# One exponential in seven computed on VectorE instead of ScalarE, with a new schedule for the background work

## The chip, the cores and the metric

The kernel runs on one core of a Trainium2 chip. The metric is device time in microseconds (us) for one execution. Engines are named as the profile names them: PE is TensorE (PEld its weight loads), ACT is ScalarE, DVE is VectorE, POOL is GpSimd. PSUM is the memory that holds PE's results. A bank is here a PSUM tile of 512 fp32 columns on 128 partitions; both kernels use eight.

## The reference

Two transformer layers on x of shape 1 x 2048 x 512 in bf16, with 32 heads of 16 columns and a feed-forward part of 1792 columns. Both layers use the same weights.

```python
x = A_x
x = x + attention(layernorm(x), A_wqkv, A_wo)   # softmax(q k^T * 16**-0.5) v, 32 heads
x = x + ffn(layernorm(x), B_w1, B_w2)           # silu between two matmuls
x = x + attention(layernorm(x), A_wqkv, A_wo)
x = x + ffn(layernorm(x), B_w1, B_w2)
```

## The kernel before

The scores of one head are cut into blocks of 128 keys x 512 queries. There are 2 layers x 4 query chunks x 4 groups x 2 parities x 16 key tiles x 4 heads = 4096 blocks. Sixty-four blocks (16 key tiles x 4 heads j) share one accumulator `o_ps`; I call them a group, so there are 64 groups. The main loop takes three blocks a step. PE computes three scores (each on one quarter of the array's rows, because a head's keys have 32 rows with padding), ACT takes the exponential of all three in one instruction, and two steps later PE multiplies the result with the values (each on one quarter of the columns).

```python
NB = 3
ps_s = tile_pool(name="ps_s", bufs=2, space=PSUM)   # 2 x 3 banks of scores
ps_o = tile_pool(name="ps_o", bufs=1, space=PSUM)   # 1 bank: the group's accumulator
ps_m = tile_pool(name="ps_m", bufs=1, space=PSUM)   # 1 bank: everything else
# ... cut ...
for t, blks in enumerate(tiles):                    # 1366 steps
    # ... ensure that q, k, v of these blocks are there ...
    s_ps = ps_s.tile([P, NB, 512], FP32, name="s_ps", tag="s")
    for i, (L, qc, g, par, kt, j) in enumerate(blks):
        nc.tensor.matmul(s_ps[:, i, :], lhsT=KT[...][r, ...], rhs=QT[L, qc][r, g, par, :], ...)
    if t >= 2:
        emit_pv(t - 2)                              # value products into o_ps
    nc.scalar.activation(p_tiles[t][...], s_ps[...], ACT.Exp, scale=SCALE)
    if urgent:
        run_urgent()                                # a finished group: divide, transpose, store
    else:
        bg.pump()                                   # one piece of background work
```

Everything else is background work: projections, output projection, layer norms and the feed-forward part are Python generators, and `bg.pump()` emits the next piece of one of them into the engines' streams. `yield None` ends a piece in the middle of a unit. `yield n` ends a unit and skips n steps before the next piece. The whole unit goes through the single `ps_m` bank.

```python
def ffn(L, c, emit):
    # ... cut ...
    for ft in range(FT):
        # four matmuls into h_ps, with `yield None` after the second
        nc.scalar.activation(t_sb[:], h_ps[:], ACT.Tanh, scale=0.5)
        nc.vector.scalar_tensor_tensor(out=hT[:, ft, :], in0=t_sb[:], scalar=1.0, in1=h_ps[:], ...)
        yield 1
    # ... the units of the other generators end with `yield 0`
```

The softmax here doesn't subtract the row's maximum and nothing guards it: scores larger than these inputs give would overflow.

## Time and profile before

| | before |
|---|---|
| time, median of 4 runs | 2280.52 us (2278.79 to 2282.66) |
| exponentials | 1366 of 1536 columns (the last of 512) |
| ACT busy | 1915.0 us, 84% |
| PE busy, mean granted clock | 1856.3 us, 0.718 |
| DVE busy | 414.4 us, 18% |

The first fence holds the busy line and the chain that ended last, from the page. The chain is followed back from the last instruction, and the line with the largest share is where time can be gained first.

```profile
PE 1856.3 (81%) x10240; PEld 537.5 (24%) x10240; DVE 414.4 (18%) x746; ACT 1915.0 (84%) x1479; POOL 36.4 (2%) x47
...
ACT 42%; PE 26%; issue 22%; DVE 9%; POOL 0%; DMA 0%; ACTq 0%; POOLq 0%; DVEq 0%
ACT p_sb L467 39%; PE s_ps L456 6%; PE o_ps L399 5%; PE h_ps L310 4%; ACT t_sb L320 3%; PE q_ps L214 2%; DVE QT L224 2%; PE f_ps L334 2%; PE v_ps L235 2%; DVE oT L408 2%; PE k_ps L197 2%; PE t_ps L177 1%; PE att L253 1%; DVE hT L321 1%; DVE st L152 1%
```

ACT, and on it the exponential, leads. The groups of before, from the page, give the busy time and mean duration of a line, then the idle time of its engine just ahead of it and what ended that.

```profile
L467 ACT ACTIVATE p_sb<-s_ps 128x1536 bf16<-128x1536 f32 x1366 | 1867.9, 1536 | 237.0 <-PE s_ps L456 235.8
L456 PE MATMUL s_ps<-QT,KT 32*128 32x512 bf16 x4096 | 705.4, 504 | 180.2 <-ACT p_sb L467 162.6
L399 PE MATMUL o_ps<-p_sb,VA 128*32 128x512 bf16 x4096 | 732.5, 514 | 42.6 <-DVE oT L408 42.3
```

ACT was busy with exponentials for 1867.9 us and stood idle 237.0 us ahead of them.

The timeline of before at a quiet place (no background work) shows PE alone. Columns are start, length, engine, line, tile.

```profile
1300.07 0.61 PE L456 MATMUL s_ps<-QT,KT 32*128 32x512 bf16 x3 [0.19 <-ACT p_sb L467]
1300.61 0.61 PE L399 MATMUL o_ps<-p_sb,VA 128*32 128x512 bf16 x3
1301.41 0.61 PE L456 MATMUL s_ps<-QT,KT 32*128 32x512 bf16 x3 [0.18 <-ACT p_sb L467]
```

Three scores take one slot of 0.54 us (start to start) together, three products another, and then PE waits for ACT. ACT sets the pace at 1.34 us a step. PE runs these in the order in which the program emits them: in the whole trace of before, three scores and three products alternate (1362 and 1363 times), apart from the first steps and the last. The view in stretches gives busy time of each engine and the granted clock: the two attention loops (first to last finished group of a layer), then a quiet stretch of five groups.

```profile
113.00:1086.00 973.00, 824.38 (x4826) 235.23 (x4825) 180.60 (x320) 919.91 (x704) 13.36 (x15) 0.75 0.00 1
1222.00:2189.00 967.00, 815.19 (x4603) 229.37 (x4600) 121.90 (x226) 916.18 (x703) 3.80 (x6) 0.68 0.01 2
1253.00:1401.00 148.00, 127.15 (x659) 33.42 (x657) 6.87 (x15) 143.08 (x108) 0.00 (x0) 0.50 0.00 1
```

The columns are the stretch, its length, busy us (and instructions) of PE, PEld, DVE, ACT and POOL, then the granted PE clock, DMA share and GB/s. In the quiet stretch PE is granted half its clock.

### The profile page before, as it was taken

How to read it: one execution, taken by the hardware profiler on the slowest of the kernel's cores; microseconds unless marked ns; L12 is line 12 of the kernel's file. 1: busy time of each engine (PE TensorE's matmuls, PEld its weight loads, DVE VectorE, ACT ScalarE, POOL GpSimd, SP SyncE). 2: the span in 40 equal slices, each digit the busy share in tenths (PEclk: the TensorE clock that was granted, in tenths of full speed). 3: DMA queues.
4: the chain of work that ended last, by engine and by line, in shares of the span. 5: the costliest groups of instructions: out<-in, count | busy, mean ns of one | idle time of the engine just before them, and what ended most of it. 6: DMA issues, size and time to landing. Idle time of an engine off the chain costs nothing.

```text
span 2279.7 us, 24321 instructions
## 1 busy us (share of the span) xinstructions
PE 1856.3 (81%) x10240; PEld 537.5 (24%) x10240; DVE 414.4 (18%) x746; ACT 1915.0 (84%) x1479; POOL 36.4 (2%) x47
## 2 busy tenths in 40 slices
PE   5788888888888888788657888878888788888866
PEld 1222222222222222222222222222222222222222
DVE  4430012130312112120221000311012100210021
ACT  1499999999899989999407999899989899999941
POOL 1100000000000000000000000000000000000000
PEclk9995567985779767985666555799567965787556
DMA  4000000000000000000000000000000000000000
GB/s 138 0 1 1 1 1 1 1 1 1 1 1 1 1 1 1 1 1 1 1 0 1 1 1 1 1 1 10 1 1 1 8 3 1 1 1 10 1 0 9
DMA packets 7917, 11.51 MB, mean 5 GB/s; under 512 B 384, under 2 KB 6784, under 8 KB 7808
## 3 DMA queue, kind: packets, MB, share of 16 engines
q1 hardware_dynamic: 7808, 9.96, 1.3%
q8 instruction: 80, 1.31, 0.2%
q14 instruction: 29, 0.24, 0.0%
HBM read 7.86 MB, written 2.10 MB: 4 GB/s over the span
## 4 chain that ended last, share of the span: by engine, by line
ACT 42%; PE 26%; issue 22%; DVE 9%; POOL 0%; DMA 0%; ACTq 0%; POOLq 0%; DVEq 0%
ACT p_sb L467 39%; PE s_ps L456 6%; PE o_ps L399 5%; PE h_ps L310 4%; ACT t_sb L320 3%; PE q_ps L214 2%; DVE QT L224 2%; PE f_ps L334 2%; PE v_ps L235 2%; DVE oT L408 2%; PE k_ps L197 2%; PE t_ps L177 1%; PE att L253 1%; DVE hT L321 1%; DVE st L152 1%
## 5 line engine op out<-in xcount | busy, mean ns | idle before, releaser
L467 ACT ACTIVATE p_sb<-s_ps 128x1536 bf16<-128x1536 f32 x1366 | 1867.9, 1536 | 237.0 <-PE s_ps L456 235.8
L456 PE MATMUL s_ps<-QT,KT 32*128 32x512 bf16 x4096 | 705.4, 504 | 180.2 <-ACT p_sb L467 162.6
L399 PE MATMUL o_ps<-p_sb,VA 128*32 128x512 bf16 x4096 | 732.5, 514 | 42.6 <-DVE oT L408 42.3
L456 PEld LDWEIGHTS <-KT 32*128 32x128 bf16 x4096 | 222.7, 95 | 724.7 <-issue 707.3
L399 PEld LDWEIGHTS <-VA 128*32 128x32 bf16 x4096 | 144.9, 98 | 500.2 <-issue 500.2
L310 PE MATMUL h_ps<-fT,w_sb 128*128 128x512 bf16 x448 | 171.1, 486 | 62.8 <-DVE hT L321 60.2
L408 DVE CAST oT<-o_ps 128x512 bf16<-128x512 f32 x64 | 44.1, 689 | 755.9 <-PE o_ps L399 755.5
L320 ACT ACTIVATE t_sb<-h_ps 128x512 f32<-128x512 f32 x112 | 73.5, 657 | 105.9 <-PE h_ps L310 105.9
L321 DVE SCALAR_TENSOR_TENSOR hT<-t_sb,h_ps 128x512 bf16<-128x512 f32 x112 | 77.0, 688 | 389.1 <-ACT t_sb L320 389.1
L334 PE MATMUL f_ps<-w_sb,hT 128*128 128x512 bf16 x448 | 129.6, 394 | 10.7 <-DVE hT L321 4.8
L310 PEld LDWEIGHTS <-w_sb 128*128 128x128 bf16 x448 | 39.3, 109 | 146.5 <-issue 142.2
L224 DVE TENSOR_SCALAR QT<-q_ps,mask 128x512 bf16<-128x512 f32 x64 | 45.1, 746 | 142.4 <-PE q_ps L214 142.4
L177 PE MATMUL t_ps<-ident,xn 128*128 128x128 bf16 x256 | 36.2, 308 | 38.7 <-DVE xn L163 33.2
L235 PE MATMUL v_ps<-w_qkv,xnT 128*128 128x512 bf16 x128 | 51.7, 530 | 18.4 <-DVE VA L244 12.7
L343 DVE SCALAR_TENSOR_TENSOR x_sb<-f_ps,x_sb 128x512 bf16<-128x512 f32 x32 | 22.1, 692 | 216.6 <-PE f_ps L334 216.6
L214 PE MATMUL q_ps<-xnT,w_qkv 128*128 128x512 bf16 x128 | 48.4, 470 | 14.9 <-DVE QT L224 13.8
L253 PE MATMUL att<-ident,oT 128*128 128x128 bf16 x256 | 34.8, 281 | 30.4 <-DVE hT L321 11.2
L197 PE MATMUL k_ps<-xnT,w_qkv 128*128 128x512 bf16 x128 | 46.3, 463 | 10.3 <-DVE xnT L182 3.9
L334 PEld LDWEIGHTS <-hT 128*128 128x128 bf16 x448 | 32.6, 99 | 67.8 <-issue 52.3
L289 PE MATMUL y_ps<-wo_sb,aT 128*128 128x512 bf16 x128 | 43.0, 427 | 4.6 <-DVE aT L283 1.6
L152 DVE BATCH_NORM_STATS2 st<-x_sb 128x6 f32<-128x512 bf16 x64 | 42.7, 667 | 3.1 <-DMA x_sb<-in_A_x_dram 3.1
L253 PEld LDWEIGHTS <-oT 128*128 128x128 bf16 x256 | 20.8, 120 | 88.0 <-issue 65.1
(30 smaller groups left out, 319.9 us busy)
## 6 DMA issues: line engine op xcount, KB each, us to landing
w_sb<-in_B_w_dram SPq DMA_DIRECT2D x2, 1792.0 KB, 14.2
x_sb<-in_A_x_dram SPq DMA_DIRECT2D x4, 512.0 KB, 8.8
out_dram<-x_sb SPq DMA_DIRECT2D x16, 128.0 KB, 1.7
w_qkv<-in_A_wqkv_dram SPq DMA_DIRECT2D x1, 1536.0 KB, 7.4
wo_sb<-in_A_wo_dram SPq DMA_DIRECT2D x1, 512.0 KB, 9.5
```

The source lines that it names most:

```text
L197: nc.tensor.matmul(k_ps[:], lhsT=w_qkv[:, ct, D + P * g : D + P * (g + 1)], rhs=xnT[L, c][:, ct, :], start=(ct == 0), stop=(ct == CT - 1),)
L214: nc.tensor.matmul(q_ps[:], lhsT=w_qkv[:, ct, P * g : P * (g + 1)], rhs=xnT[L, c][:, ct, :], start=(ct == 0), stop=(ct == CT - 1),)
L224: nc.vector.tensor_scalar_mul(out=QT[L, c][:, g, par, :], in0=q_ps[:], scalar1=masks[par][:, 0:1])
L235: nc.tensor.matmul(v_ps[:], lhsT=xnT[L, c][:, ct, tq * P : (tq + 1) * P], rhs=w_qkv[:, ct, 2 * D : 3 * D], start=(ct == 0), stop=(ct == CT ...
L310: nc.tensor.matmul(h_ps[:], lhsT=w1_sb[:, ct, ft * P : (ft + 1) * P], rhs=fT[:, ct, :], start=(ct == 0), stop=(ct == CT - 1),)
L320: nc.scalar.activation(t_sb[:], h_ps[:], ACT.Tanh, scale=0.5)
L321: nc.vector.scalar_tensor_tensor(out=hT[:, ft, :], in0=t_sb[:], scalar=1.0, in1=h_ps[:], op0=ALU.add, op1=ALU.mult,)
L334: nc.tensor.matmul(y_ps[:], lhsT=hT[:, ft, tq * P : (tq + 1) * P], rhs=w2_sb[:, ft, :], start=(ft == 0), stop=(ft == FT - 1),)
L399: nc.tensor.matmul(o_ps[32 * j : 32 * j + 32, :], lhsT=VA[L, kt // 4][:, kt % 4, 17 * h : 17 * h + 32], rhs=p_sb[:, i, :], start=(kt == 0) ...
L408: nc.vector.tensor_copy(out=oT[:], in_=o_ps[:])
L456: nc.tensor.matmul(s_ps[:, i, :], lhsT=KT[L, kt // 4][r, g, (kt % 4) * P : (kt % 4 + 1) * P], rhs=QT[L, qc][r, g, par, :], start=True, sto ...
L467: nc.scalar.activation(p_tiles[t][:, 0:n, :].rearrange("p a b -> p (a b)"), s_ps[:, 0:n, :].rearrange("p a b -> p (a b)"), ACT.Exp, scale= ...
```

## The change

The intent is to take exponentials off ACT. In a step with three ACT blocks a fourth block now goes to DVE, as long as it lies before place 54 of its group. That makes 9 of 64 blocks, 576 in all. The code uses no exponential instruction on DVE; it builds the exponential out of the number format. An affine writes 1024 (x + const), with x the score in units of log2, into uint16. Read as fp16 these bits are y = 2^e (1+m), where x = e + m. Two bitwise ops cut out 2^e (as fp16) and r = 1+m. Then r (A + C r^2) 2^e, added to 2^e, is close to a constant times 2^x. The addition is not done on DVE: PE accumulates both parts with the same values, in two value products.

The fourth block needs a PSUM bank. The kernel keeps to eight, so the score tiles shrink from 3+3 to 3+2 banks and the exponentials alternate between three blocks and two. Apart from this the schedule of the background work changes: units skip a step, a further step lies between the matmuls of h and their tanh, a finished group is divided one step later, the queries of the next chunk are projected group by group, and the background piece is emitted ahead of the step's exponential instead of after it. The sizes of some buffer pools change too (queries, x, tanh).

```diff
-    NB = 3
+    D_LAST = 54
-    ps_s = ctx.enter_context(tc.tile_pool(name="ps_s", bufs=2, space=bass.MemoryType.PSUM))
+    ps_s = ctx.enter_context(tc.tile_pool(name="ps_s", bufs=1, space=bass.MemoryType.PSUM))
@@ every generator but the layer norm
-        yield 0
+        yield 1
@@ ffn
+            yield None
             t_sb = tpool.tile([P, 512], FP32, name="t_sb", tag="t")
             nc.scalar.activation(t_sb[:], h_ps[:], ACT.Tanh, scale=0.5)
@@ steps
-    tiles = [blocks[i : i + NB] for i in range(0, len(blocks), NB)]
+        n = 3 - len(steps) % 2
+        a = blocks[pos : pos + n]
+        pos += n
+        d = blocks[pos : pos + 1] if n == 3 and pos % 64 < D_LAST else []
@@ the moved block: emit_d, then one stage of step_d a step (cut)
+        s_ps = ps_s.tile([P, 512], FP32, name="d_ps", tag="sd")
+        score(blk, s_ps[:])
+        nc.vector.tensor_scalar(out=pr["y"][...], in0=s_ps[:], scalar1=..., scalar2=..., op0=mult, op1=add)
+            nc.vector.tensor_scalar(out=rf.bitcast(I32), in0=y.bitcast(I32), scalar1=0x03FF03FF, scalar2=0x3C003C00, op0=bitwise_and, op1=bitwise_or)
+            nc.vector.tensor_scalar(out=ef.bitcast(I32), in0=y.bitcast(I32), scalar1=0x7C007C00, op0=bitwise_and)
+                nc.vector.tensor_tensor(out=rf, in0=rf, in1=rf, op=ALU.mult)
+                nc.vector.tensor_scalar(out=rf, in0=rf, scalar1=EXP_C, scalar2=EXP_A, op0=ALU.mult, op1=ALU.add)
+                nc.vector.tensor_tensor(out=rf, in0=rf, in1=y.bitcast(FP16), op=ALU.mult)
@@ value products of a moved block: two, the e part and the r part
+                    blk, [pr["e"][:, i, :].bitcast(FP16), pr["r"][:, i, :].bitcast(FP16)]
@@ main loop
+            run_d()
+            if not run_urgent(t):
+                bg.pump()
             p_tiles[t] = ppool.tile(...)
             nc.scalar.activation(...)
-            if urgent:
-                run_urgent()
-            else:
-                bg.pump()
```

More of the change, by code (lines that the diff above doesn't have):

```diff
@@ L1 @@
+import math
 from collections import deque
@@ L13 @@
 FP32 = mybir.dt.float32
+FP16 = mybir.dt.float16
+U16 = mybir.dt.uint16
+I32 = mybir.dt.int32
 BF16 = mybir.dt.bfloat16
@@ L87 @@
     VW = 17 * H + 16
-    NB = 3
+    EXP_K = 4.58045666e-01
+    SHIFT = -math.log2(EXP_K)
+    EXP_A = 4.65708474e-01 / EXP_K
+    EXP_C = 7.62931392e-02 / EXP_K
+    D_LAST = 54
     const = ctx.enter_context(tc.tile_pool(name="const", bufs=1))
@@ L94 @@
     vpool = ctx.enter_context(tc.tile_pool(name="vpool", bufs=7))
-    qpool = ctx.enter_context(tc.tile_pool(name="qpool", bufs=2))
-    xtpool = ctx.enter_context(tc.tile_pool(name="xtpool", bufs=5))
+    qpool = ctx.enter_context(tc.tile_pool(name="qpool", bufs=6))
+    xtpool = ctx.enter_context(tc.tile_pool(name="xtpool", bufs=4))
     ftpool = ctx.enter_context(tc.tile_pool(name="ftpool", bufs=1))
     xnpool = ctx.enter_context(tc.tile_pool(name="xnpool", bufs=4))
-    ppool = ctx.enter_context(tc.tile_pool(name="ppool", bufs=4))
+    ppool = ctx.enter_context(tc.tile_pool(name="ppool", bufs=2))
+    dpool = ctx.enter_context(tc.tile_pool(name="dpool", bufs=2))
     opool = ctx.enter_context(tc.tile_pool(name="opool", bufs=2))
@@ L102 @@
     hpool = ctx.enter_context(tc.tile_pool(name="hpool", bufs=1))
-    tpool = ctx.enter_context(tc.tile_pool(name="tpool", bufs=2))
+    tpool = ctx.enter_context(tc.tile_pool(name="tpool", bufs=1))
     small = ctx.enter_context(tc.tile_pool(name="small", bufs=3))
-    ps_s = ctx.enter_context(tc.tile_pool(name="ps_s", bufs=2, space=bass.MemoryType.PSUM))
+    ps_s = ctx.enter_context(tc.tile_pool(name="ps_s", bufs=1, space=bass.MemoryType.PSUM))
     ps_o = ctx.enter_context(tc.tile_pool(name="ps_o", bufs=1, space=bass.MemoryType.PSUM))
@@ L206, in proj_k @@
         nc.vector.tensor_copy(out=KT[L, c][:, g, :], in_=k_ps[:])
-        yield 0
+        yield 1
     def proj_q(L, c, g):
-        if g == 0:
-            QT[L, c] = qpool.tile([P, NG, 2, 512], BF16, name="QT", tag="QT")
+        QT[L, c, g] = qpool.tile([P, 2, 512], BF16, name="QT", tag="QT")
         q_ps = ps_m.tile([P, 512], FP32, name="q_ps", tag="m")
@@ L224, in proj_q @@
             nc.vector.tensor_scalar_mul(
-                out=QT[L, c][:, g, par, :], in0=q_ps[:], scalar1=masks[par][:, 0:1]
+                out=QT[L, c, g][:, par, :], in0=q_ps[:], scalar1=masks[par][:, 0:1]
             )
-        yield 0
+        yield 1
     def proj_v(L, c):
@@ L247, in proj_v @@
             )
-            yield 0
+            yield 1
     def group_out(L, qc, g, par, oT):
@@ L283, in out_proj @@
             nc.vector.tensor_copy(out=aT[:], in_=a_ps[:])
-            yield 0
+            yield 1
             for u in range(2):
@@ L300, in out_proj @@
                 )
-                yield 0
+                yield 1
     def ffn(L, c, emit):
@@ L352, in ffn @@
                 nc.sync.dma_start(of[tt * P : (tt + 1) * P, :], x_sb[:, tt, :])
-            yield 0
+            yield 1
     def add_qkv(L, c):
@@ L359, in add_qkv, with next_q @@
         bg.add(("v", L, c), proj_v(L, c))
-    def add_q(L, c):
-        for g in range(NG):
+    def next_q(L, c, g):
+        L, c = (L, c + 1) if c + 1 < NC else (L + 1, 0)
+        if L < 2:
             bg.add(("q", L, c, g), proj_q(L, c, g))
@@ L374 @@
     blocks = list(stream())
-    tiles = [blocks[i : i + NB] for i in range(0, len(blocks), NB)]
-    o_tiles = {}
+    steps = []
+    pos = 0
+    while pos < len(blocks):
+        n = 3 - len(steps) % 2
+        a = blocks[pos : pos + n]
+        pos += n
+        d = blocks[pos : pos + 1] if n == 3 and pos % 64 < D_LAST else []
+        pos += len(d)
+        steps.append((a, d))
+    o_tiles = {}
+    o_count = {}
+    o_total = {}
+    for a, d in steps:
+        for blk, m in [(b, 1) for b in a] + [(b, 2) for b in d]:
+            o_total.setdefault(blk[0:4], [0] * 4)[blk[5]] += m
     p_tiles = {}
+    pairs = deque()
     def start_chunk(L, qc):
         attn[L, qc] = apool.tile([P, 4, D], BF16, name="attn", tag="attn")
-        if qc + 1 < NC and (L, qc) != (1, 0):
-            add_q(L, qc + 1)
-        if (L, qc) == (0, NC - 1):
-            add_q(1, 0)
     def finish_chunk(L, qc):
@@ L390, in finish_chunk, with pv_block @@
             add_qkv(1, qc)
-    def emit_pv(tile_i):
-        p_sb = p_tiles.pop(tile_i)
-        for i, (L, qc, g, par, kt, j) in enumerate(tiles[tile_i]):
-            if kt == 0 and j == 0:
-                o_tiles[L, qc, g, par] = ps_o.tile([P, 512], FP32, name="o_ps", tag="o")
-            o_ps = o_tiles[L, qc, g, par]
-            h = 8 * g + 2 * j + par
-            nc.tensor.matmul(
-                o_ps[32 * j : 32 * j + 32, :],
-                lhsT=VA[L, kt // 4][:, kt % 4, 17 * h : 17 * h + 32],
-                rhs=p_sb[:, i, :],
-                start=(kt == 0),
-                stop=(kt == NKT - 1),
-            )
-            if kt == NKT - 1 and j == 3:
-                oT = opool.tile([P, 512], BF16, name="oT", tag="oT")
-                nc.vector.tensor_copy(out=oT[:], in_=o_ps[:])
-                urgent.append(((L, qc, g, par), group_out(L, qc, g, par, oT)))
+    def pv_block(blk, rhs):
+        L, qc, g, par, kt, j = blk
+        h = 8 * g + 2 * j + par
+        return [((L, qc, g, par), j, VA[L, kt // 4][:, kt % 4, 17 * h : 17 * h + 32], p) for p in rhs]
@@ new lines, in emit_pv @@
+    def emit_pv(mms):
+        mms = list(mms)
+        while mms:
+            used = set()
+            for mm in list(mms):
+                key, j, lhsT, rhs = mm
+                if j in used:
+                    continue
+                used.add(j)
+                mms.remove(mm)
+                if key not in o_tiles:
+                    o_tiles[key] = ps_o.tile([P, 512], FP32, name="o_ps", tag="o")
+                    o_count[key] = [0] * 4
+                n = o_count[key]
+                n[j] += 1
+                nc.tensor.matmul(
+                    o_tiles[key][32 * j : 32 * j + 32, :],
+                    lhsT=lhsT,
+                    rhs=rhs,
+                    start=(n[j] == 1),
+                    stop=(n[j] == o_total[key][j]),
+                )
+        if o_count[key] == o_total[key]:
+            oT = opool.tile([P, 512], BF16, name="oT", tag="oT")
+            nc.vector.tensor_copy(out=oT[:], in_=o_tiles[key][:])
+            urgent.append((key, group_out(*key, oT), step_now[0] + 1))
@@ new lines, in emit_d @@
+    def emit_d(blk):
+        s_ps = ps_s.tile([P, 512], FP32, name="d_ps", tag="sd")
+        score(blk, s_ps[:])
+        if not pairs or len(pairs[-1]["blks"]) == 2 or pairs[-1]["last"]:
+            pairs.append(
+                dict(
+                    blks=[],
+                    stage=0,
+                    last=False,
+                    y=dpool.tile([P, 2, 512], U16, name="d_y", tag="y"),
+                )
+            )
+        pr = pairs[-1]
+        nc.vector.tensor_scalar(
+            out=pr["y"][:, len(pr["blks"]), :],
+            in0=s_ps[:],
+            scalar1=float(1024 * SCALE * math.log2(math.e)),
+            scalar2=float(1024 * (15 - SHIFT)),
+            op0=ALU.mult,
+            op1=ALU.add,
+        )
+        pr["blks"].append(blk)
+        pr["last"] = 4 * blk[4] + blk[5] + 6 >= D_LAST
@@ new lines, in step_d @@
+    def step_d(pr):
+        n = len(pr["blks"])
+        y = pr["y"][:, 0:n, :].rearrange("p a b -> p (a b)")
+        if pr["stage"] == 0:
+            e = dpool.tile([P, 2, 512], U16, name="d_e", tag="e")
+            r = dpool.tile([P, 2, 512], U16, name="d_r", tag="r")
+            pr["e"], pr["r"] = e, r
+            ef = e[:, 0:n, :].rearrange("p a b -> p (a b)")
+            rf = r[:, 0:n, :].rearrange("p a b -> p (a b)")
+            nc.vector.tensor_scalar(
+                out=rf.bitcast(I32),
+                in0=y.bitcast(I32),
+                scalar1=0x03FF03FF,
+                scalar2=0x3C003C00,
+                op0=ALU.bitwise_and,
+                op1=ALU.bitwise_or,
+            )
+            nc.vector.tensor_scalar(
+                out=ef.bitcast(I32),
+                in0=y.bitcast(I32),
+                scalar1=0x7C007C00,
+                scalar2=None,
+                op0=ALU.bitwise_and,
+            )
+        else:
+            rf = pr["r"][:, 0:n, :].rearrange("p a b -> p (a b)").bitcast(FP16)
+            if pr["stage"] == 1:
+                nc.vector.tensor_tensor(out=rf, in0=rf, in1=rf, op=ALU.mult)
+                nc.vector.tensor_scalar(
+                    out=rf, in0=rf, scalar1=EXP_C, scalar2=EXP_A, op0=ALU.mult, op1=ALU.add
+                )
+            else:
+                nc.vector.tensor_tensor(out=rf, in0=rf, in1=y.bitcast(FP16), op=ALU.mult)
+        pr["stage"] += 1
@@ new lines, in run_d, with ready_d @@
+    def run_d():
+        for pr in pairs:
+            if pr["stage"] > 0 or len(pr["blks"]) == 2 or pr["last"]:
+                if pr["stage"] < 3:
+                    step_d(pr)
+                else:
+                    pr["stage"] += 1
+    def ready_d():
+        mms = []
+        while pairs and pairs[0]["stage"] >= 4:
+            pr = pairs.popleft()
+            for i, blk in enumerate(pr["blks"]):
+                mms += pv_block(
+                    blk, [pr["e"][:, i, :].bitcast(FP16), pr["r"][:, i, :].bitcast(FP16)]
+                )
+        return mms
@@ L411, with score @@
+    def score(blk, out):
+        L, qc, g, par, kt, j = blk
+        r = slice(32 * j, 32 * j + 32)
+        nc.tensor.matmul(
+            out,
+            lhsT=KT[L, kt // 4][r, g, (kt % 4) * P : (kt % 4 + 1) * P],
+            rhs=QT[L, qc, g][r, par, :],
+            start=True,
+            stop=True,
+        )
     urgent = deque()
+    step_now = [0]
     with tc.manual_schedule(
@@ L427, with run_urgent @@
             bg.add(("q", 0, 0, g), proj_q(0, 0, g))
-        def run_urgent():
-            bg.close()
-            while urgent:
-                key, gen = urgent.popleft()
-                for _ in gen:
-                    pass
-                bg.done.add(("g",) + key)
-                L, qc, g, par = key
-                if (g, par) == (NG - 1, 1):
-                    finish_chunk(L, qc)
-                    if (L, qc) == (0, NC - 1):
-                        add_q(1, 1)
-        for t, blks in enumerate(tiles):
-            for L, qc, g, par, kt, j in blks:
+        def run_urgent(t):
+            if not urgent or bg.inside or urgent[0][2] > t:
+                return False
+            key, gen, _ = urgent.popleft()
+            for _ in gen:
+                pass
+            L, qc, g, par = key
+            if (g, par) == (NG - 1, 1):
+                finish_chunk(L, qc)
+            return True
+        late = []
+        for t, (a_blks, d_blks) in enumerate(steps):
+            for L, qc, g, par, kt, j in a_blks + d_blks:
                 if (g, par, kt, j) == (0, 0, 0, 0):
                     start_chunk(L, qc)
+                if (par, kt, j) == (0, 0, 0) and (L, qc, g) != (0, 0, 0):
+                    pg = (L * NC + qc) * NG + g - 1
+                    next_q(pg // (NC * NG), pg // NG % NC, pg % NG)
                 if j == 0 and kt % 4 == 0:
@@ L452 @@
                         bg.ensure(("v", L, c))
-            s_ps = ps_s.tile([P, NB, 512], FP32, name="s_ps", tag="s")
-            for i, (L, qc, g, par, kt, j) in enumerate(blks):
-                r = slice(32 * j, 32 * j + 32)
-                nc.tensor.matmul(
-                    s_ps[:, i, :],
-                    lhsT=KT[L, kt // 4][r, g, (kt % 4) * P : (kt % 4 + 1) * P],
-                    rhs=QT[L, qc][r, g, par, :],
-                    start=True,
-                    stop=True,
-                )
-            if t >= 2:
-                emit_pv(t - 2)
-            n = len(blks)
-            p_tiles[t] = ppool.tile([P, NB, 512], BF16, name="p_sb", tag="p")
+            n = len(a_blks)
+            size = 3 - t % 2
+            s_ps = ps_s.tile([P, size, 512], FP32, name="s_ps", tag=f"s{size}")
+            for i, blk in enumerate(a_blks):
+                score(blk, s_ps[:, i, :])
+            for blk in d_blks:
+                emit_d(blk)
+            step_now[0] = t
+            mms, late = late, []
+            if t >= 0:
+                mms += ready_d()
+                for u in (t - 2,):
+                    if u >= 0:
+                        p_sb = p_tiles.pop(u)
+                        for i, blk in enumerate(steps[u][0]):
+                            mms += pv_block(blk, [p_sb[:, i, :]])
+            if mms:
+                key = min(mm[0] for mm in mms)
+                late = [mm for mm in mms if mm[0] != key]
+                emit_pv([mm for mm in mms if mm[0] == key])
+            run_d()
+            if not run_urgent(t):
+                bg.pump()
+            p_tiles[t] = ppool.tile([P, size, 512], BF16, name="p_sb", tag=f"p{size}")
             nc.scalar.activation(
@@ L472 @@
             )
-            if urgent:
-                run_urgent()
-            else:
-                bg.pump()
-        for t in range(len(tiles) - 2, len(tiles)):
-            emit_pv(t)
-        run_urgent()
+        t = len(steps)
+        while p_tiles or late:
+            step_now[0] = t
+            mms, late = late, []
+            for u in sorted(p_tiles):
+                p_sb = p_tiles.pop(u)
+                for i, blk in enumerate(steps[u][0]):
+                    mms += pv_block(blk, [p_sb[:, i, :]])
+            emit_pv(mms)
+        bg.close()
+        while urgent:
+            run_urgent(t + 2)
         while bg.queue:
```

## The prediction

> **What bounds it now.** The exponential on ACT. The page's busy table gives ACT 1915.0 us of 2279.7 (84%), PE 1856.3 (81%), DVE 414.4 (18%); the chain that ended last gives 39% to the p_sb exponential. In the timeline, ten back-to-back 128x1536 exponentials take 13.61 us, so 1361 ns each: about 427 ns per 512-column block plus 81 ns per instruction. The view in stretches shows ACT near 94% busy in the two attention loops (about 104–1103 us and 1210–2188 us, some 1977 us in all, 30.9 us per group of 64 blocks). The remaining ~303 us (start-up, the layer boundary, the last feed-forward) have ACT mostly idle, waiting for PE/DVE chains.
>
> **What changes.** From the built programs: 576 of the 4096 blocks (9 per 64) leave ACT. DVE does them instead: a 512-wide affine from PSUM each, then in 320 batches (256 of two blocks, 64 of one) two bitwise ops, two multiplies, one multiply-add. Each moved block needs two value matmuls, so PE gets 576 more (10240 to 10816). ACT runs 1408 exponentials (704 of three blocks, the rest of two or fewer) instead of 1366. Background work is equal, spaced wider; the order shows it still finishing before the layer boundary (184 matmuls in one run there, 176 before) and the same 164 at the end.
>
> **Cost.** ACT, estimated: 3520 x 427 + 1408 x 81 = 1617 us, against 1859: 242 us saved, 3.8 us per group (25.3 us, 26 with tanh).
> DVE: the affine as the 128x512 PSUM cast, 0.69 us. For the SBUF ops the Trainium skill ("VectorE: DVE Perf Modes", the perf-mode tier table and the side-by-side) gives about 150 fixed cycles plus one cycle per 4 elements (16-bit tensor_scalar), per 2 (32-bit tensor_scalar, 16-bit tensor_tensor). The trace agrees where comparable: xn, 128x512 bf16 with two pointers, median 405 ns; the PSUM copy of 1024 bf16 takes 692 ns, as the cast of 512 fp32. Estimate: bitwise 0.43, multiplies 0.70, multiply-add 0.43 us, so ~4.0 us per pair, ~2.4 per single: ~1190 us added, DVE busy ~1550–1620 us. Per group 18.6 + ~5.5 background = 24 of 26 us: nearly full.
> PE: groups of 3 scores or value products take 0.32 us at full clock, 0.54 at half; row or column groups run together, so a fourth score is almost free, while the doubled products cost an extra round per batch, 320 x 0.2–0.4 = 70–130 us of PE, mostly hidden.
>
> **On the path.** About 240 us of exponential come off it. I expect 70–100 us back: where background runs, DVE demand in the moved part of a group (about 22–24 us against 21.4 of ACT) delays PE at the single d_ps and ps_m banks, and PE is in order, so the next scores come late. The 303 us outside stay, +5.
>
> **Predicted: 2105 us, 80% range 2035 to 2190.** Faster by over 2%: 0.88; within 2%: 0.08; slower: 0.04.
>
> **Checks.** ACT exponential busy 1600–1650 us; 1024-wide ones ~935 ns apart; DVE busy 1500–1700 us with ops as estimated; PE s_ps/d_ps waits on DVE appear; mean PE clock rises from 0.72; ACT idle before p_sb grows per group from ~1.2 us to 2–3; boundary gap about 106–115 us still there.
>
> **What would make it wrong.** The 16-bit multiplies or the bitwise ops at one element per cycle (+160 to +340 us DVE): then DVE bounds the loop, 2150–2250. DVE finishing easily and PE warm throughout: 2040. Late moved products stalling PE in order every group: above 2190.

## More of the kernel before

The waits of before show two that PE has for DVE inside the loop; both matter later.

```profile
PE h_ps L310 <- DVE hT L321: 60.2, 75, 1.4
...
PE o_ps L399 <- DVE oT L408: 42.3, 42, 2.4
```

In the loops ACT is idle 973.00 - 919.91 + 967.00 - 916.18 = 103.9 us.

## The result, and the profile after

The changed kernel took 2054.49 us (median of 8 runs, 2045.04 to 2061.41), with a correct result. Before took 2282.28 us (median of 13 runs, 2278.43 to 2284.87). The ratio is 0.9001 (95% interval 0.8984 to 0.9017). Ratios here and below are the mean time of a kernel's fast runs over the mean of before's fast runs of the same rounds, so they are not quite the ratios of the medians quoted.

The busy line and the chain of after, from the page:

```profile
PE 1687.2 (82%) x10816; PEld 511.6 (25%) x10816; DVE 1464.1 (71%) x2922; ACT 1685.5 (82%) x1521; POOL 37.2 (2%) x47
...
PE 35%; DVE 27%; ACT 26%; issue 11%; POOL 0%; DMA 0%; ACTq 0%; POOLq 0%; DVEq 0%
```

ACT is busy 229.5 us less, and the span is 226.5 us shorter (2279.7 to 2053.2). PE has 576 matmuls more and yet is busy 169 us less. The chain is now shared by three engines. The groups of after, shapes apart:

```profile
L601 ACT ACTIVATE p_sb<-s_ps 128x1536 bf16<-128x1536 f32 x704 | 1059.9, 1506 | 156.8 <-PE d_ps L524 144.8 <-PE s_ps L524 6.2 <-ACT p_sb L601 2.1
L601 ACT ACTIVATE p_sb<-s_ps 128x1024 bf16<-128x1024 f32 x704 | 757.7, 1076 | 79.0 <-PE s_ps L524 77.4
...
L457 DVE TENSOR_SCALAR d_y<-d_ps 128x512 uint16<-128x512 f32 x576 | 395.4, 686 | 267.7 <-PE d_ps L524 265.3
...
L495 DVE TENSOR_TENSOR d_r<-d_r 128x1024 f16<-128x1024 f16 x256 | 174.8, 683 | 0.0
L500 DVE TENSOR_TENSOR d_r<-d_r,d_y 128x1024 f16<-128x1024 f16 x256 | 174.4, 681 | 0.0
...
L477 DVE TENSOR_SCALAR d_r<-d_y 128x512 int32<-128x512 int32 x256 | 110.7, 432 | 8.8
L496 DVE TENSOR_SCALAR d_r<-d_r 128x1024 f16<-128x1024 f16 x256 | 110.5, 432 | 8.9
L485 DVE TENSOR_SCALAR d_e<-d_y 128x512 int32<-128x512 int32 x256 | 107.4, 420 | 0.0
```

Every DVE op has the length that was estimated for it, within 3%. The waits of after that answer to those shown before, and the one that the prediction named:

```profile
PE h_ps L318 <- DVE hT L330: 36.6, 26, 1.4
...
PE d_ps L524 <- DVE d_y L457: 7.8, 15, 2.0
...
PE o_ps L432 <- DVE oT L441: 4.5, 6, 0.7
```

Both old waits of PE for DVE shrank, by 23.6 and 37.8 us, though DVE has three and a half times the work. The stretches of after: a quiet stretch (the same five groups as before), then the two loops.

```profile
1146.00:1276.00 130.00, 103.30 (x719) 32.15 (x717) 94.56 (x191) 125.92 (x111) 0.00 (x0) 0.89 0.00 1
...
119.00:984.00 865.00, 757.22 (x5111) 223.97 (x5109) 685.71 (x1373) 808.62 (x725) 13.75 (x15) 0.93 0.00 1
1121.00:1963.00 842.00, 716.09 (x4893) 215.27 (x4892) 637.40 (x1285) 805.88 (x724) 3.80 (x6) 0.93 0.01 3
```

ACT's idle time in the loops is 865.00 - 808.62 + 842.00 - 805.88 = 92.5 us, where before had 103.9. The granted clock in the quiet stretch went from 0.50 to 0.89. The timeline of after, on PE, in such a stretch:

```profile
1204.31 0.39 PE L432 MATMUL o_ps<-d_e,VA 128*32 128x512 f16 x2
1204.32 0.39 PE L432 MATMUL o_ps<-p_sb,VA 128*32 128x512 bf16 x2
1204.61 0.39 PE L432 MATMUL o_ps<-d_r,VA 128*32 128x512 f16 x2
1204.84 0.38 PE L432 MATMUL o_ps<-p_sb,VA 128*32 128x512 bf16 x1
1205.15 0.39 PE L524 MATMUL s_ps<-QT,KT 32*128 32x512 bf16 x2
1205.47 0.39 PE L432 MATMUL o_ps<-p_sb,VA 128*32 128x512 bf16 x2
1205.81 0.39 PE L524 MATMUL s_ps<-QT,KT 32*128 32x512 bf16 x3
1205.82 0.39 PE L524 MATMUL d_ps<-QT,KT 32*128 32x512 bf16 x1
1206.14 0.40 PE L432 MATMUL o_ps<-p_sb,VA 128*32 128x512 bf16 x3
```

The fourth score starts 0.01 us after the other three. Where scores and products alternate, a slot of two, three or four matmuls takes 0.31 to 0.34 us start to start here, at the full clock, where it took 0.54 us before. Product rounds in a row lie closer (1204.61 to 1204.84: 0.23 us).

So the time came in at the size of the ACT saving with nothing given back. I had expected 70 to 100 us to be given back, and had given the new schedule no value of its own. The experiments ask which of the two was wrong.

### The profile page after: what moved, and what is told of

It is laid out like the page before. It is cut to its first block, busy times and chain, and to the rows that moved or that the text cites. A ratio compares the mean times of both kernels' runs of the same rounds, so it can differ in the third digit from the quotient of the medians.

```text
span 2053.2 us, 27736 instructions
## 1 busy us (share of the span) xinstructions
PE 1687.2 (82%) x10816; PEld 511.6 (25%) x10816; DVE 1464.1 (71%) x2922; ACT 1685.5 (82%) x1521; POOL 37.2 (2%) x47
## 4 chain that ended last, share of the span: by engine, by line
PE 35%; DVE 27%; ACT 26%; issue 11%; POOL 0%; DMA 0%; ACTq 0%; POOLq 0%; DVEq 0%
ACT p_sb L601 25%; PE o_ps L432 11%; PE s_ps L524 9%; PE f_ps L343 5%; DVE d_y L457 5%; PE h_ps L318 3%; DVE d_r L495 3%; PE v_ps L243 2%; DVE d_r L477 2%; DVE d_r L496 2%; DVE QT L232 2%; DVE st L161 2%; DVE d_r L500 2%; DVE d_e L485 2%; ACT t_sb L329 2%
## 5 line engine op out<-in xcount | busy, mean ns | idle before, releaser
L601 ACT ACTIVATE p_sb<-s_ps 128x1536 bf16<-128x1536 f32 (+1 forms) x1408 | 1647.2, 1291 | 235.9 <-PE d_ps L524 144.8
L457 DVE TENSOR_SCALAR d_y<-d_ps 128x512 uint16<-128x512 f32 x576 | 395.4, 686 | 267.7 <-PE d_ps L524 265.3
L524 PE MATMUL d_ps<-QT,KT 32*128 32x512 bf16 x576 | 234.4, 407 | 8.5 <-DVE d_y L457 7.8
L500 DVE TENSOR_TENSOR d_r<-d_r,d_y 128x1024 f16<-128x1024 f16 (+1 forms) x320 | 201.5, 630 | 1.7
L495 DVE TENSOR_TENSOR d_r<-d_r 128x1024 f16<-128x1024 f16 (+1 forms) x320 | 201.6, 630 | 0.0
L318 PE MATMUL h_ps<-fT,w_sb 128*128 128x512 bf16 x448 | 155.7, 448 | 38.2 <-DVE hT L330 36.6
L432 PE MATMUL o_ps<-d_r,VA 128*32 128x512 f16 x576 | 136.6, 422 | 8.7 <-DVE d_r L500 8.7
L343 PE MATMUL f_ps<-w_sb,hT 128*128 128x512 bf16 x448 | 130.7, 392 | 13.2 <-DVE attn L268 5.7
L496 DVE TENSOR_SCALAR d_r<-d_r 128x1024 f16<-128x1024 f16 (+1 forms) x320 | 133.5, 417 | 11.1
L432 PE MATMUL o_ps<-d_e,VA 128*32 128x512 f16 x576 | 136.6, 423 | 0.0
L477 DVE TENSOR_SCALAR d_r<-d_y 128x512 int32<-128x512 int32 (+1 forms) x320 | 129.0, 403 | 8.8
L485 DVE TENSOR_SCALAR d_e<-d_y 128x512 int32<-128x512 int32 (+1 forms) x320 | 125.8, 393 | 0.0
```

The costliest lines, as they stand in the source:

```text
L318: nc.tensor.matmul(h_ps[:], lhsT=w1_sb[:, ct, ft * P : (ft + 1) * P], rhs=fT[:, ct, :], start=(ct == 0), stop=(ct == CT - 1),)
L343: nc.tensor.matmul(y_ps[:], lhsT=hT[:, ft, tq * P : (tq + 1) * P], rhs=w2_sb[:, ft, :], start=(ft == 0), stop=(ft == FT - 1),)
L432: nc.tensor.matmul(o_tiles[key][32 * j : 32 * j + 32, :], lhsT=lhsT, rhs=rhs, start=(n[j] == 1), stop=(n[j] == o_total[key][j]),)
L457: nc.vector.tensor_scalar(out=pr["y"][:, len(pr["blks"]), :], in0=s_ps[:], scalar1=float(1024 * SCALE * math.log2(math.e)), scalar2=float( ...
L477: nc.vector.tensor_scalar(out=rf.bitcast(I32), in0=y.bitcast(I32), scalar1=0x03FF03FF, scalar2=0x3C003C00, op0=ALU.bitwise_and, op1=ALU.bi ...
L485: nc.vector.tensor_scalar(out=ef.bitcast(I32), in0=y.bitcast(I32), scalar1=0x7C007C00, scalar2=None, op0=ALU.bitwise_and,)
```

## The experiments

Each kernel was run on one chip beside before, one look and three timed rounds (five for the last). Diffs are against the changed kernel unless another is named.

| run | what | median us | ratio to before (95% interval) | clock of the profiled run |
|---|---|---|---|---|
| after | the change | 2054.49 | 0.9001 (0.8984 to 0.9017) | 0.892 |
| a1_sched | schedule only, no block moved, 3+3 banks | 2204.64 | 0.9667 (0.9652 to 0.9683) | 0.764 |
| a2_split | schedule and 3/2 split, no block moved | 2346.72 | 1.0322 (1.0255 to 1.0389) | 0.678 |
| a3_d30 | 320 blocks moved | 2214.46 | 0.9699 (0.9673 to 0.9725) | 0.809 |
| a4_dve_more | one bitwise op twice | 2124.68 | 0.9315 (0.9301 to 0.9328) | 0.871 |
| a5_dve_less | two of six DVE ops left out | 2020.56 | 0.8849 (0.8829 to 0.8869) | 0.896 |
| a6_one_product | one product for a moved block | 2071.24 | 0.9074 (0.9061 to 0.9088) | 0.827 |
| a7_old_spacing | old spacing of background work | 2245.01 | 0.9828 (0.9807 to 0.9849) | 0.855 |
| a9_split_fill | a2 with 819 idle matmuls | 2266.72 | 0.9922 (0.9896 to 0.9947) | 0.759 |
| a10_gap_only | old spacing, tanh gap kept | 2152.19 | 0.9418 (0.9390 to 0.9447) | 0.872 |
| b2_ln_spread | layer norms spread | 2059.69 | 0.9018 (0.8999 to 0.9037) | 0.899 |
| a8_d59 | 640 blocks moved | 2061.62 | 0.9033 (0.9011 to 0.9055) | 0.886 |
| b5_fill_products | 3263 idle products | 2054.01 | 0.8992 (0.8970 to 0.9014) | 0.902 |

### The schedule alone (a1_sched)

```diff
-        n = 3 - len(steps) % 2
+        n = 3
-        d = blocks[pos : pos + 1] if n == 3 and pos % 64 < D_LAST else []
+        d = blocks[pos : pos + 1] if False else []
-            size = 3 - t % 2
+            size = 3
-    ... name="ps_s", bufs=1 ...  name="ppool", bufs=2
+    ... name="ps_s", bufs=2 ...  name="ppool", bufs=4
```

> The new schedule alone: no block moved, three blocks to every exponential as before, same bank count. Theory A (the gain is exponential work taken off ACT): 2280 us within 1%, ACT busy about 1915 as before, PE clock about 0.72. Rival B (a good part of the gain comes from the wider spacing of background work and the later group finish): 2180 to 2250 us.

It took 2204.64 us, 3.3% less than before, without a single block moved. Rival B holds and theory A alone does not. Its stretches of the two loops:

```profile
112.00:1050.00 938.00, 785.17 (x4833) 232.52 (x4830) 180.81 (x321) 918.23 (x705) 13.35 (x15) 0.81 0.00 1
1187.00:2114.00 927.00, 779.80 (x4614) 224.34 (x4611) 125.50 (x231) 913.53 (x703) 3.79 (x6) 0.73 0.01 2
```

ACT does the same work as before, but is idle for 938.00 - 918.23 + 927.00 - 913.53 = 33.2 us in the loops instead of 103.9. The two waits of PE for DVE that before had are smaller, and nearly what they are in after:

```profile
PE h_ps L318 <- DVE hT L330: 36.6, 26, 1.4
...
PE o_ps L432 <- DVE oT L441: 6.7, 10, 1.1
```

This also places the change as a whole. From a1 to after, ACT loses 1831.8 - 1614.5 = 217 us of busy time in the loops, and gains 92.5 - 33.2 = 59 us of idle time. The give-back exists; the schedule had paid for it. (a1 takes the schedule as a whole; which part of it brings the 76 us in the kernel without moved blocks stays open.)

### The split alone (a2_split)

```diff
-        d = blocks[pos : pos + 1] if n == 3 and pos % 64 < D_LAST else []
+        d = blocks[pos : pos + 1] if False else []
```

> New schedule, no block moved, exponentials alternating three and two blocks: 1639 of them instead of 1366. Theory A, with 81 ns for each further instruction: 273 x 81 ns = 22 us more than the schedule alone, so about 2300 us; ACT exponential busy about 1885. Rival B: below 2260 us. Rival C (it is the PE clock that went up with shorter steps and makes the loop faster): clock well above 0.72 and time below before's.

It took 2346.72 us: 142 us more than a1, where 22 us were expected for 273 more instructions. (The profiled execution was the slowest of the four, 2378.95 us; the other three lie between 2344 and 2348.) None of the three theories expected this. The quiet stretch of a2 and that of a1:

```profile
1325.00:1477.00 152.00, 148.18 (x666) 34.32 (x665) 9.53 (x20) 145.45 (x129) 0.00 (x0) 0.51 0.00 1
```

```profile
1218.00:1363.00 145.00, 123.36 (x669) 33.23 (x666) 9.52 (x20) 142.38 (x107) 0.00 (x0) 0.55 0.00 1
```

In a2 PE has an instruction on record for 148.18 of 152 us, and is granted half its clock all the while. A slot of two matmuls lasts as long as a slot of three, and there are more slots, so PE at half clock has no slack left. In stretches with background work it falls behind:

```profile
1380.16 0.61 PE L524 MATMUL s_ps<-QT,KT 32*128 32x512 bf16 x2
1380.70 0.61 PE L432 MATMUL o_ps<-p_sb,VA 128*32 128x512 bf16 x2
1381.24 1.03 PE L222 MATMUL q_ps<-xnT,w_qkv 128*128 128x512 bf16 x2
1382.21 0.61 PE L524 MATMUL s_ps<-QT,KT 32*128 32x512 bf16 x3
1382.75 0.62 PE L432 MATMUL o_ps<-p_sb,VA 128*32 128x512 bf16 x3
1383.30 1.03 PE L222 MATMUL q_ps<-xnT,w_qkv 128*128 128x512 bf16 x2
```

Start to start, two slots of two take 1.08 us (1380.16 to 1381.24), nearly as long as two slots of three (1.09 us), and two projection matmuls take 0.97 us. Slots and projection together are 2.06 us, for an exponential of 0.93 or 1.36 us by the prediction's estimate. In the chain that ended last PE has 61% in a2, and 24% in a1. So freeing the bank for the moved block costs 142 us when nothing is moved, and moving the 576 blocks then brings 2346.72 - 2054.49 = 292 us, more than the estimate for the exponentials it takes away (1882 us for 1639 exponentials by the 427 ns and 81 ns of the prediction, less 1617: 265 us).

### Is it the clock? (a9_split_fill, a6_one_product)

a9 takes the split kernel and lets PE compute, in every step of three, one more score on the row group that stands idle. It goes into the bank that the moved block would use, and nothing reads it. The result stays correct.

```diff
-            for blk in d_blks:
-                emit_d(blk)
+            if n == 3:
+                js = {b[5] for b in a_blks}
+                f_ps = ps_s.tile([P, 512], FP32, name="fill_ps", tag="sd")
+                score(a_blks[0][:5] + (({0, 1, 2, 3} - js).pop(),), f_ps[:])
```

> The split kernel without moved blocks (2347 us, clock 0.678), plus 819 score matmuls on the unused row group into the spare bank, never read; result correct. Theory C (a fuller array is granted a higher clock, and the low clock cost the split some 120 us): clock 0.75 to 0.9 and faster than the split, 2230 to 2320 us. Rival F (more matmuls only add PE work; the clock follows something else): clock 0.66 to 0.70 and 2345 to 2420 us.

With 819 useless matmuls more the kernel took 2266.72 us, 80 us less, and the clock went from 0.678 to 0.759 (over all runs, 0.678 to 0.701 in a2 and 0.746 to 0.766 in a9). Rival F falls. The gain is not in the quiet stretch (clock 0.52, and the groups as long as in a2) but where there is background work: over the same three groups (the 51st to the 53rd finished) a2 needs 99 us at clock 0.81 and a9 92 us at 0.98 (first line a2, second a9):

```profile
1836.30:1935.40 99.10, 93.67 (x495) 23.30 (x496) 15.79 (x26) 93.84 (x87) 0.00 (x0) 0.81 0.02 6
1745.00:1837.20 92.20, 79.31 (x525) 24.23 (x533) 15.77 (x26) 92.08 (x87) 0.00 (x0) 0.98 0.02 6
```

a6 goes the other way, from after: one product for a moved block instead of two. Its output is wrong, which doesn't matter for the time. The count of products that closes a group is changed to match (cut).

```diff
-                    blk, [pr["e"][:, i, :].bitcast(FP16), pr["r"][:, i, :].bitcast(FP16)]
+                    blk, [pr["r"][:, i, :].bitcast(FP16)]
```

> Wrong result on purpose: one value product for a moved block instead of two, so 576 matmuls less, DVE work the same. Theory E1 (PE work of the extra rounds is on the path): 20 to 70 us faster, 1985 to 2035. Rival C (the extra products fill the array and hold the granted clock up): clock below 0.87 and 2055 to 2110 us. Hidden: 2045 to 2060.

With 576 matmuls less it took 2071.24 us, 17 us more, at clock 0.827 instead of 0.892. The intervals of the two ratios do not touch. Its quiet stretch:

```profile
1152.00:1287.00 135.00, 119.57 (x672) 28.82 (x672) 94.78 (x192) 128.75 (x111) 0.00 (x0) 0.68 0.00 1
```

That is 135 us for the five groups at clock 0.68, where after needs 130 us at 0.89. The second product is not merely hidden: with it the kernel is faster. The quiet stretches line up by matmuls recorded per us:

| quiet stretch of | matmuls / us | PE busy share | granted clock |
|---|---|---|---|
| a2_split | 666/152 = 4.4 | 97% | 0.51 |
| before | 659/148 = 4.5 | 86% | 0.50 |
| a1_sched | 669/145 = 4.6 | 85% | 0.55 |
| a9_split_fill | 730/152 = 4.8 | 96% | 0.52 |
| a6_one_product | 672/135 = 5.0 | 89% | 0.68 |
| after | 719/130 = 5.5 | 79% | 0.89 |
| b5_fill_products | 970/128 = 7.6 | 78% | 0.93 |

From a6 down the table the clock rises with the matmuls per us; above, it does not follow them (a9 has more than a1 and a lower clock). A faster clock also raises matmuls per us, so the table alone proves no cause. a9 and a6, where only matmuls were added or taken away, do show that clock and time of the whole run follow, though in a9 the quiet stretch hardly moved (0.51 to 0.52).

The clock record in the traces says more. It has two values, full and half, in stretches of 3.41 us and multiples of it. In before, a1 and a2 together, all 127 recorded steps down followed a stretch of 3.41 us with PE busy on record for at most 73% of it, and 126 of 127 steps up followed one with PE busy for at least 99.5%. But 371 stretches at half clock were as full, and only those 126 led to a step up. Nor does the number of matmuls tell these apart: in a2 the 33 that led to a step up have 11 matmuls at the median, the other 182 have 14. So gaps in PE's work go with the clock too, and a rival is untested: the added matmuls may act by closing such gaps and not by filling the array. The rule of the throttle is not settled by this.

### More and less work on DVE (a4_dve_more, a5_dve_less)

```diff
@@ a4: the second bitwise op stands twice (same result)
+            nc.vector.tensor_scalar(out=ef.bitcast(I32), in0=y.bitcast(I32), scalar1=0x7C007C00, ...)
```

> One of the two bitwise ops done twice (same result): about 0.4 us more of DVE for each of 320 batches, some 120 us of DVE busy time. Theory A (DVE has slack, 29% idle): 2050 to 2075 us. Theory of the prediction (DVE demand in the moved part holds up PE at the single d_ps and m banks): 60 to 120 us more, 2115 to 2175.

It took 2124.68 us, 70 us more, for 123 us more DVE busy time (1464.1 to 1587.1). The prediction's theory holds: with 29% of DVE idle, its time is still on the path. The table of waits does not show how. The wait of PE for the bank of the moved block only rose to 13.2 us:

```profile
PE d_ps L531 <- DVE d_y L457: 13.2, 22, 2.0
```

Meanwhile the clock fell to 0.871, and in one quiet group (28.5 us against 25.5, the largest difference of the five) to 0.70 from 0.93. The five quiet groups together took 136.8 us at 0.83, against 130.0 at 0.89. A small delay on DVE that costs PE its clock would explain both, but that link is only argued.

```diff
@@ a5: square and multiply-add left out, result wrong on purpose
-                nc.vector.tensor_tensor(out=rf, in0=rf, in1=rf, op=ALU.mult)
-                nc.vector.tensor_scalar(out=rf, in0=rf, scalar1=EXP_C, scalar2=EXP_A, ...)
+                pass
```

> Wrong result on purpose: square and multiply-add left out of the moved blocks, so about 335 us less DVE busy, all else equal. Theory D (DVE delay is what gives back about 71 us of ACT idle in the changed kernel): 1980 to 2015 us, DVE busy about 1130, ACT idle before the exponential down from 236 to about 170. Rival E (the idle comes from PE: two score groups and two product groups for five blocks, at whatever clock is granted): 2035 to 2060.

It took 2020.56 us, 34 us less, between the two expectations, with DVE busy 1175.2 us and ACT's idle time ahead of the exponential 205.5 us instead of 235.9. In the loops ACT's idle time fell from 92.5 to 66.6 us. So the ops left out, 289 us of DVE busy time, account for 26 us of the 59 given back. The groups with a layer norm gained most: the nine that took 29 us or more in after (29.2 to 33.2, the layer boundary aside) took 27.7 to 31.1. (The comparison with the reference passed this kernel although its exponentials are wrong. It is a measurement, not a version to use.)

### The spacing inside the changed kernel (a7_old_spacing, a10_gap_only)

```diff
@@ a7: every generator but the layer norm and the first part of ffn
-        yield 1
+        yield 0
@@ a7: ffn (a10 keeps this line)
-            yield None
             t_sb = tpool.tile([P, 512], FP32, name="t_sb", tag="t")
```

> The changed kernel with the background work spaced as before (no skipped step after a unit, no gap before the tanh), later group finish and per-group queries kept. If the 76 us that the schedule alone gained come from the spacing: 2095 to 2150 us, with PE waits for hT and oT and ACT idle up. If they come from the later group finish and the query order: 2045 to 2075.

It took 2245.01 us: without the new spacing the change is worth 1.7%. The loss of 190 us is larger than any expectation. One wait stands out, here ahead of the same wait of after:

```profile
ACT t_sb L328 <- PE h_ps L318: 200.4, 110, 26.9
```

```profile
ACT t_sb L329 <- PE h_ps L318: 110.6, 28, 27.3
```

In the changed kernel the background piece stands ahead of the step's exponential. Without the further step ACT reaches the tanh before PE has finished h, 110 times instead of 28, and the exponential behind it waits too. This part was made by the new order of emission, so a7 is not before's schedule. a10 therefore puts that one line back.

> The changed kernel with the old spacing, but with the step before the tanh kept. The kernel without either took 2245 us and ACT waited 95 us more for h_ps before the tanh. If the missing gap before the tanh is the main cost of that run: 2070 to 2130 us, wait of t_sb for h_ps back to about 110 us. If the skipped step after each unit is: 2170 to 2230 us.

It took 2152.19 us, between the two expectations. The wait for h is back at the size it has in after (108.0 us, 28 times). So the gap before the tanh is worth 93 us and the skipped steps 98 us. The groups show where the skipped steps count: the first of each chunk, with the output projection and the next layer norm, take 35 to 37 us in a10 and 27 to 28 us in after. In one of these (1368.1 to 1404.7 us in a10, 1303.7 to 1330.6 in after) DVE is busy 28.27 of 36.6 us and PE is granted 0.80; in after DVE is busy 24.20 of 26.9 us and PE is granted 1.00. (Part of this work only moves: with the next group, a10 takes 66.2 us and after 58.5.) I read this as packed background work and moved blocks wanting DVE at once, and everything in order behind them slipping; no run separates it further.

### The dose, and attempts to go further (a3_d30, a8_d59, b2_ln_spread, b5_fill_products)

```diff
-    D_LAST = 54
+    D_LAST = 30        # a3: 320 blocks moved; a8 has 59: 640 blocks moved
```

> 320 blocks moved instead of 576 (5 of 64), 1511 exponentials. Theory A: linear in ACT work, 3776 x 427 + 1511 x 81 ns = 1735 us of exponential, 118 us more than the changed kernel, so about 2170 us (2150 to 2190). A theory with DVE as the limit of the changed kernel: much less than 118 us lost, 2080 to 2130.

It took 2214.46 us, above the expected range of 2150 to 2190. From a2 over a3 to after, 0, 320 and 576 moved blocks give 2346.72, 2214.46 and 2054.49 us: 0.41 us for each of the first 320 blocks and 0.62 us for each of the next 256. The estimate from ACT work alone is 0.46 us a block throughout. The second half brings more than it takes off ACT, and the clock rises with it (0.678, 0.809, 0.892).

> 640 blocks moved (10 of 64, the last at 55 to 58), 1383 exponentials: 64 x 427 + 25 x 81 ns = 29 us less on ACT, about 120 us more on DVE. ACT-bound: 2020 to 2035 us. DVE-bound or late products holding the one o_ps bank at the group's end: 2060 to 2110 us.

It took 2061.62 us, just where the second theory's range begins and 0.3% above after by the medians; the intervals of the ratios only just overlap. ACT's exponentials fell to 1614.3 us, and its idle time ahead of them rose from 235.9 to 265.2. PE's wait for the one `o_ps` bank came back:

```profile
PE o_ps L432 <- DVE oT L441: 38.3, 45, 2.0
```

So the limit of 54 is about as far as it goes: 33 us of exponential less bring nothing. The returned wait fits, but does not prove, the theory that the last moved block's products now hold the accumulator at the group's end.

```diff
@@ b2, layer norm: one statistics pair a step, one normalisation a step
-            if i == 1:
-                yield 0
+            if i < 3:
+                yield 1
@@
-        yield 0
+            yield 0          # inside the loop over the four tiles
```

> The changed kernel with the layer norms spread: one statistics pair a step with a skipped step after it, one normalisation a step. The slow groups of the changed kernel (31 to 33 us against 26 to 28) are those with a layer norm, and they fell to 28 to 30 with less DVE work. Theory D (bursts of DVE work delay the moved blocks and so PE): those groups 28 to 30 us, in all 2015 to 2040 us. If DVE bursts do not matter: 2050 to 2065.

It took 2059.69 us, a miss. The group in which the first feed-forward layer norm lies did fall from 32.1 to 28.0 us, as expected, but others rose (three from about 26.5 to 30.5, 31.8 and 31.7), and ACT's idle time ahead of the exponential stayed at 240.6 us. I read this as collisions moved and not removed.

```diff
@@ b5, after each round of value products
+            for f in range(4):
+                if f not in used and 0 < n[f] < o_total[key][f]:
+                    nc.tensor.matmul(o_tiles[key][32 * f : 32 * f + 32, :], lhsT=zero_w[:], rhs=rhs, start=False, stop=False)
```

> The changed kernel plus 3263 value products with zero weights on column groups that stand idle in a round (result unchanged), 30% more matmuls. Theory C (a fuller array is granted more clock, and clock still costs the changed kernel time): clock 0.93 or more, 2015 to 2045 us. If clock no longer limits it, or idle groups filled do not count: 2045 to 2065. If the matmuls cost PE time: 2070 to 2150 us.

It took 2054.01 us, equal to after, with a correct result and 30% more matmuls. Its clock hardly rose: 0.891 to 0.902 over its runs, 0.882 to 0.904 in after; in the quiet stretch 0.93 against 0.89, for 128 us instead of 130. So these matmuls bring nothing, but the run does not show whether a higher clock would still save time, nor whether products with zero weights count for the throttle like others. No run with the right exponentials was clearly faster than after.

## Why the prediction was right or wrong

The time was right: 2054.49 us lies in the range of 2035 to 2190, 50 us below the centre. The balance behind it was partly wrong, and that the range held was in part luck. The terms as written sum to 2280 - 240 + 70 to 100 + 5 = 2115 to 2145 us (the text does not say why the centre is lower). The measured time is 61 to 91 us below that sum, about what the schedule is worth, which was left out; the range was wide enough to cover it.

- **The exponentials leave ACT: right.** 242 us predicted; in the loops 217 us left ACT from a1 to after. The measured exponential time of 1647 us lies in the range of 1600 to 1650. Back to back in after, a 1536-wide one starts the next after 1331 ns and a 1024-wide one after 904 ns (medians): 427 ns a block, as estimated.
- **The DVE ops: right.** The affine, the multiplies, the multiply-add and the bitwise ops were estimated at 0.69, 0.70, 0.43 and 0.43 us and measured at 0.686, 0.683 and 0.681, 0.432, 0.432 and 0.420. The trace agrees with the Trainium skill, "VectorE: DVE Perf Modes", the perf-mode tier table. The groups sum to 1187 us (1190 predicted). The busy time of the engine came out lower (1464 us, predicted 1500 to 1700) because consecutive ops overlap: in the groups their ends are counted twice.
- **"I expect 70-100 us back": right in kind, near in size, hidden.** Against the kernel with the same schedule, 59 us of idle time came back in the loops. a4 and a5 show that DVE work takes part (26 of the 59 us in a5). But the wait named for it, PE at d_ps, measures only 7.8 us; it is not where the loss can be read.
- **"Background work is equal, spaced wider": the step that failed.** It entered the sum with zero. It measures 76 us as a1, without any moved block, and the spacing is worth 190 us inside the changed kernel (a7). This term is why the idle time per group did not grow from 1.2 to 2-3 us as stated: on the loops it went from 103.9/62 = 1.7 to 92.5/62 = 1.5, while a1 has 33.2/62 = 0.5. The waits for hT and oT that it shortens stood in the profile of before.
- **The doubled products, "mostly hidden": wrong sign.** Taking them away costs 17 us (a6). Clock above 0.72 was predicted as a symptom; a9 and a6 make it a part of the cause, though how the matmuls raise it stays open.
- **The split into 3 and 2 was costed by its instructions only**, 42 more in the changed kernel. Alone it costs 142 us (a2): 22 us by the estimate for its instructions, 80 us that a9 gets back at a higher clock, and 40 us that no run separates. In the changed kernel the moved blocks fill the slots, and together with them the split pays.
- **The parts outside the loops stayed**, as predicted: the group across the layer boundary takes 136.4 us after and 135.8 before.

## What to carry to other kernels

When a change moves work and reorders the rest, run the reordering alone: here it was a third of the gain (76 of 228 us), and the changed kernel without its spacing was worth only 1.7% (a7). On an engine that issues in order, short pieces with a step between them can be worth more than the work they delay. And ask how full a matmul slot is before cutting it: a slot of two quarter-array matmuls took as long as one of three (0.54 us at half clock in a2), so more and emptier slots left PE without slack.

## What the Trainium skill lacked or had wrong

- "TensorE: Matmul & The Clock Gate", "What's actually happening", has the throttle set by how busy PE has been recently. The steps down agree: all 127 in before, a1 and a2 followed 3.41 us with PE busy for at most 73%. But a busy record is not enough: in a2 PE was on record as busy for 148.18 of 152 us and was granted 0.51 (the ends of matmuls are modelled in the record). Adding matmuls on idle quarters of the array (a9, 819 of them) raised the clock of the whole run from 0.678 to 0.759; taking 576 away (a6) lowered it from 0.892 to 0.827. The page does not say what counts as busy when small matmuls share the array.
- "ScalarE: Activation LUTs", "Rules for kernel authors", calls ScalarE the only option for `exp`. Six DVE ops (4.0 us for 1024 columns by the sum of their measured lengths, two affines included) and a second value product did it here, with a result that passed the comparison (as a5's wrong exponentials did) and, together with the new schedule, 10% less time.
- No page gives the time of packed slots that alternate between row groups (scores) and column groups (products): 0.54 us start to start at half clock, 0.31 to 0.34 us at the full one, for two to four matmuls; product rounds in a row lie 0.23 us apart.
